# Two-layer attention and gMLP kernel: another order of the start, key features held in SBUF, and small works of a step in another place

## The chip, the cores and the metric

The kernel runs on one core of a Trainium2 chip. The metric is the device time of one execution in microseconds (us); smaller is better. TensorE (PE) multiplies matrices, VectorE (DVE), ScalarE (ACT) and GpSimd (POOL) do elementwise work, SyncE (SP) issues the DMA transfers. PSUM is where TensorE writes.

## What is computed

Two layers, one after the other, each the pair below, with the same weights: a memory-augmented attention and a gMLP mixer, both on a layer-normed input and added to the residual.

```
x = A_x                                     # 1 x 2048 x 640
twice:
    x = x + attention(layernorm(x))
    x = x + gmlp(layernorm(x))

attention: q, k, v = x @ wq, x @ wk, x @ wv      # 32 heads of 20
    M, z = 0, 0
    for s in 4 segments of 512 rows:
        a_dot = softmax(q k^T * 20^-0.5, causal) @ v
        a_mem = (phi(q) @ M) / (phi(q) @ z + 1e-6)    # phi(t) = t + 1 if t > 0 else exp(t)
        o_s = g * a_mem + (1 - g) * a_dot             # g = sigmoid(beta)
        M += phi(k)^T v;  z += sum phi(k)
    return o @ wo

gmlp: z = gelu(x @ w_in)                         # 640 -> 2 x 864
    z1, z2 = halves;  z2 = layernorm(z2)
    g = w_sp @ z2 + b_sp                         # w_sp 2048 x 2048
    return (z1 * g) @ w_out                      # 864 -> 640
```

## The kernel before

**Precision.** A float32 product is done in three fp16 matmuls: each operand is split into a high and a low half (names end in `h` and `l`, or `hl` for both), and high x high, high x low and low x high are added in PSUM. Weights are first scaled by a power of two taken from their largest magnitude: DVE finds the maxima (`wamk`, `wam`), TensorE turns them (`wtp`, L60) and spreads the result over the partitions (`wbc`, L67), and DVE makes the inverse scale `iv` from it (L69 to L74). A split is then an ACT instruction for the high half (L81) and a DVE instruction for the low one (L82), five of each for a weight of 640 rows.

**Stages of the profiled run.** The start, 0 to 60 us (load, scale and split w_v, w_q, w_k; layer norm of the first rows; the first segment's values, L1052; the first unit of queries and keys); attention of layer 0 to about 592; the mixer's first product, L412, and its halves to about 800; the mixer's large product over rows to about 1130; then attention and mixer again to the end.

**Rows.** A tile `t` of 128 rows is prepared by `prep`: load (L1014), statistics (L305 to L308), the subtraction and scaling (L1033), an ACT cast and a low half into `xnhl` (L320, L321), and a DMA that transposes it into `xt` (L322). `value(t)` makes 30 matmuls out of it, in two PSUM tiles `vps`.

**Units.** A unit is six heads (120 columns) of a segment. `unit(s, m)` makes 15 matmuls for its queries (`qps`) and 15 for its keys (`kps`, L1111). `out` then takes the result out of PSUM: the high half (L1125, ACT), the low half (L1129, DVE), both sent to a stack in HBM by DMA (L1226, L1227), from which the scores' operands `qk` are read; and the features phi: `relu` (L1128, ACT), exp written back to the same PSUM bank (L1138, ACT), and the minimum with one plus `relu` (L1143, DVE, for keys; L1141 for queries). Keys' features are split into `phl` (L1152, L1153), transposed by DMA (L1156, `pk`) and go into the memory update `mup` (L1209); DVE masks this into `mst` (L1215). The memory read `num` (L1180) multiplies query features by `mst`. PSUM tiles of values, projections, queries and keys share two banks; the memory's products and the transposed maxima share one more, and the sums `pv` have another.

**Scores.** For a pair of heads TensorE makes scores `mp` for the row maxima (L1246, L1255), DVE reduces them (`mxs`, L1316, L1319), TensorE makes the scores again with the maxima taken off (`es`), ACT takes the exponential into `P` or `Pb` (L1293), ACT casts its high half `PH` (L1328), POOL makes the low half `PL` (L1332), and TensorE multiplies with the values (`pv`, L1366). DVE divides and adds to the memory's part `gm` (L1377 to L1390), and the finished rows go out as `ohl` (L1402).

**Order.** In the attention TensorE's order is written out by steps: `Attention.run` draws matmuls from generators (scores, values `v`, units by their number, projections `p`) in the order of a plan, one list for each segment:

```
plan = ["1v2v3v4v0", "1234vvvv0p", "1p234vvvv0", "1p2p34pppppppp"]
```

`post(k, f)` puts the work of another engine `f` into the list of `k` steps later, in the order of the calls. On the other engines a scheduler sets the order, steered by priorities and by `issue_after`. Each engine runs its own list in order, and SP's transfers share one queue.

Of the kernel before, what the change touches and what calls it, by code (L numbers as in the profile page):

```python
# [19 lines left out]
L = S // NSEG  # L20
# [161 lines left out]
def prologue(g, ctx, wv, wq, wk, wo, w_in, w_out):  # L182
# [7 lines left out]
    with tc.tile_pool(name="wpro", bufs=1, side="right", reuse_waits="tile") as p, \  # L190
# [5 lines left out]
        with tc.high_priority(offset=HP):  # L196
            am = p.tile([128, KD], F32, name="wamk")
            for k in range(KD):
                nc.vector.tensor_reduce(am[:, k:k + 1], st[:, k], AX.X, ALU.max, apply_absolute_value=True)
            nc.vector.tensor_reduce(g.wam[:, 0:1], am, AX.X, ALU.max)  # L200
# [3 lines left out]
        for k in range(KD):  # L204
            e = split_scaled(g, g.w["v"][0][:, k], g.w["v"][1][:, k], st[:, k], 0)
            if k == 2:
                g.third = e
    g.qk_w = wq, wk


def query_key_weights(g, stage, pool, psum, tag):

    nc, tc = g.nc, g.tc
    st = []
    for w, x in zip(g.qk_w, "hl"):
        parts = [g.top[1].tile([128, 2160], F32, tag=f"wi1{x}", name=f"wst{x}1")[:, :3 * D].rearrange("p (k c) -> p k c", c=D),
                 g.top[0].tile([128, 1600], F32, tag=f"wo{x}", name=f"wst{x}2")[:, :2 * D].rearrange("p (k c) -> p k c", c=D)]
        st.append([parts[k // 3][:, k % 3] for k in range(KD)])
        for k in range(KD):
            nc.sync.dma_start(st[-1][k], w[k * 128:(k + 1) * 128, :])  # L220
    for i, nm in ((1, "q"), (2, "k")):
        with tc.issue_after(g.vscale.ins):
            am = pool.tile([128, KD], F32, tag="wamk", name="wamk")
            for k in range(KD):
                nc.vector.tensor_reduce(am[:, k:k + 1], st[i - 1][k], AX.X, ALU.max, apply_absolute_value=True)
# [6 lines left out]
        for k in range(KD):  # L232
            split_scaled(g, h[:, k], l[:, k], st[i - 1][k], i)
        yield

# [102 lines left out]
def phase1b(g, o_d, x, x1_d, z1_d, zh, zl):  # L338

    nc, tc = g.nc, g.tc  # L340
    with ExitStack() as ctx:
# [4 lines left out]
        if not g.wsp_scaled:  # L346
            nc.sync.dma_start(g.bsp, g.b_sp.rearrange("(t p) -> p t", p=128))
        g.wi[0].paired(wp0)
# [68 lines left out]
        g.loaded, g.gelu, g.lo = {}, {}, {}  # L417
# [33 lines left out]
        with tc.high_priority(offset=3 * HP2):  # L451
            a = load(0)
        with tc.high_priority(offset=HP2):
            xn = attn_out(0, *a)
            a = load(ORDER[1])
            th = xn_t(*xn)
        for i, t in enumerate(ORDER):
# [3 lines left out]
            if i + 1 < NT:  # L461
                xn = attn_out(ORDER[i + 1], *a)
# [402 lines left out]
def attn_consts(g, cp, beta):  # L865
# [6 lines left out]
    with tc.tile_pool(name="tmp", bufs=1) as tp, tc.tile_pool(name="acp", bufs=1, space=PSUM) as pp:  # L872
        f = tp.tile([128, 192], F32, name="fmask")
        for t, n, b, sg, op in ((g.eye, 64, 0, 1, ALU.not_equal), (g.step["q"], 192, -64, 1, ALU.is_ge), (g.step["k"], 192, 64, -1, ALU.is_ge)):
            nc.vector.memset(f, 0.0)
            for h in range(2):
                v = f[64 * h:64 * h + 64, :n]
                nc.gpsimd.affine_select(v, v, [[sg, n]], op, BIG if op is ALU.not_equal else -BIG, base=b, channel_multiplier=-sg)
            nc.vector.tensor_copy(t, f[:, :n])
# [7 lines left out]
        nc.vector.tensor_scalar(g.gate, g.gate, 1.0, 0.125, ALU.add, ALU.mult)  # L887

# [29 lines left out]
class Attention:  # L918
# [9 lines left out]
    def __init__(self, g, x, o_d, x1_d):  # L928
# [8 lines left out]
        self.now, self.later, self.half, self.rd = None, {}, {}, set()  # L937
        self.lead = []

    def post(self, k, f, c=None, into=None):  # L940
# [7 lines left out]
        (self.later if into is None else into).setdefault(t, []).append(f)  # L948
# [60 lines left out]
    def prep(self, t):  # L1009
# [4 lines left out]
        nc.sync.dma_start(xt, self.x[t])  # L1014
        ln = []

        def behind():
            ctx = ExitStack()
            for e in (g.hold[:2] or (g.third,)) if t > 1 else ():
# [11 lines left out]
        def last():  # L1031
            mv, rs = ln
            nc.vector.tensor_scalar(xt, xt, mv[:, 0:1], rs, ALU.subtract, ALU.mult)  # L1033
            hl = self.e2.tile([128, 2, D], F16, tag="xh", name="xnhl")
            e = split_t(g, hl, self.xt[s % 2][:, :, :, c], xt, low=nc.vector if g.hold and t in (2, 3) else nc.gpsimd)
            if t == 3:
# [4 lines left out]
    def value(self, t):  # L1041
# [5 lines left out]
        for n in range(2):  # L1047
# [8 lines left out]
            def out(ps=ps.rearrange("p (h d) -> p h d", d=DH), v=self.vs[s % 2][:, t % 4, n * 16:(n + 1) * 16, :]):  # L1056
                nc.scalar.mul(v[:, :, 0:DH], ps, QS)
                nc.vector.scalar_tensor_tensor(v[:, :, DH + 1:], ps, QS, v[:, :, 0:DH], ALU.mult, ALU.subtract)
# [38 lines left out]
    def unit(self, s, m):  # L1097
# [3 lines left out]
        for nm in "qk" if s else "kq":  # L1101
# [12 lines left out]
            self.out(nm, s, m, ps)  # L1114
# [3 lines left out]
    def out(self, nm, s, m, ps):  # L1118
# [18 lines left out]
        def features(r):  # L1137
            nc.scalar.activation(ps, ps, AF.Exp, scale=g.rq if q else g.rk)  # L1138
# [3 lines left out]
            else:  # L1142
                nc.vector.scalar_tensor_tensor(r, ps, 1.0, r, ALU.min, ALU.add)  # L1143
# [54 lines left out]
    def update(self, s, m):  # L1198
# [20 lines left out]
        self.post(1, out)  # L1219

    def stack(self, nm, s, m, hl):
# [6 lines left out]
        if nm == ("k" if s else "q"):  # L1228
# [93 lines left out]
    def cast(self, n, h):  # L1322
# [7 lines left out]
        def low(engine):  # L1330
            for c in (slice(0, 640), slice(640, 1280))[::-1 if n % 2 and h else 1]:
                engine.tensor_tensor(PL[:, c], P[:, h, c], PH[:, c], ALU.subtract)  # L1332

        if h == 0 or n < self.N - self.TAIL:
# [341 lines left out]
```

## Time and profile before

| | |
|---|---|
| runs | 2218.08, 2218.99, 2214.55 us; median 2218.08 |
| profiled execution | 2217.2 us, its span 2215.5 us |
| mean clock granted to TensorE | 0.991 of full speed |
| TensorE busy | 2087.8 us (94%) |
| DVE, ACT, POOL busy | 1625.6, 1250.9, 1402.7 us (73, 56, 63%) |

The span is the time of the profiled execution from the first to the last recorded instruction; some 1.7 us lie around it. A row of the waits gives engine, tile and line that waited, who ended the wait, the total in us, how many times, and the longest. A row of the timeline gives start, duration, engine, line, operation, output and inputs with their shapes, and in brackets the idle time before it and what ended that.

### The profile page before, as it was taken

How to read it: one execution, taken by the hardware profiler on the slowest of the kernel's cores; microseconds unless marked ns; L12 is line 12 of the kernel's file. 1: busy time of each engine (PE TensorE's matmuls, PEld its weight loads, DVE VectorE, ACT ScalarE, POOL GpSimd, SP SyncE). 2: the span in 40 equal slices, each digit the busy share in tenths (PEclk: the TensorE clock that was granted, in tenths of full speed). 3: DMA queues.
4: the chain of work that ended last, by engine and by line, in shares of the span. 5: the costliest groups of instructions: out<-in, count | busy, mean ns of one | idle time of the engine just before them, and what ended most of it. 6: DMA issues, size and time to landing. Idle time of an engine off the chain costs nothing.

```text
span 2215.5 us, 53079 instructions
## 1 busy us (share of the span) xinstructions
PE 2087.8 (94%) x21322; PEld 1265.2 (57%) x21322; DVE 1625.6 (73%) x2889; ACT 1250.9 (56%) x1641; POOL 1402.7 (63%) x1172
## 2 busy tenths in 40 slices
PE   5998888999899999999999989989999999999999
PEld 3555655666545555555555556656665555555555
DVE  7788788788587758888657787787875764675563
ACT  4588788788644433333326987878884433333331
POOL 3387898788645345566414889888894433674660
PEclk9999999999999999999999999999999999999999
DMA  6666557344776686666455456553455335876752
GB/s 177 163 174 184 133 163 197 96 121 126 185 199 182 162 278 171 170 183 178 137 167 131 112 139 153 126 118 90 123 141 145 106 110 185 217 175 171 177 142 82
DMA packets 537703, 342.79 MB, mean 155 GB/s; under 512 B 411600, under 2 KB 463312, under 8 KB 537456
## 3 DMA queue, kind: packets, MB, share of 16 engines
q1 hardware_dynamic: 537456, 339.39, 57.2%
q8 instruction: 167, 2.74, 0.5%
q14 instruction: 80, 0.66, 0.1%
HBM read 159.18 MB, written 92.55 MB: 114 GB/s over the span
## 4 chain that ended last, share of the span: by engine, by line
PE 67%; DVE 14%; ACT 7%; issue 4%; DMA 4%; POOL 3%; SPq 1%; ACTq 0%; DVEq 0%; POOLq 0%
PE ga L670 12%; PE zp L412 11%; PE cyp L706 7%; PE pv L1366 4%; PE qps L1111 4%; PE vps L1052 3%; PE gb L670 3%; PE mp L1255 3%; PE yps L1084 3%; DVE mxs L1319 3%; PE gc L670 3%; PE gd L670 3%; PE kps L1111 2%; PE es L1255 2%; ACT PH L1328 2%
## 5 line engine op out<-in xcount | busy, mean ns | idle before, releaser
L1332 POOL TENSOR_TENSOR PL<-P,PH 128x640 f16<-128x640 f32 x384 | 535.1, 1422 | 86.7 <-PE pv L1366 67.9
L1319 DVE TENSOR_REDUCE mxs<-mp 128x2 f32<-128x1024 f32 (+2 forms) x384 | 320.2, 861 | 123.4 <-PE mp L1246 121.3
L1293 ACT ACTIVATE P<-es,sc 128x1024 f32<-128x1024 f32 (+1 forms) x256 | 271.6, 1061 | 102.0 <-PE es L1246 95.8
L640 POOL TENSOR_TENSOR ts<-ts,wt 128x512 f32<-128x512 f32 x196 | 283.3, 1457 | 11.0
L412 PEld LDWEIGHTS <-th 128*128 128x128 f16 x1920 | 188.0, 98 | 169.6 <-issue 6.9
L1328 ACT CAST PH<-P 128x1280 f16<-128x1280 f32 x192 | 239.7, 1249 | 2.5 <-PE pv L1366 1.0
L670 PEld LDWEIGHTS <-wts 128*128 128x128 f16 x1536 | 150.2, 98 | 134.0 <-issue 5.5
L670 PE MATMUL ga<-zh,wts 128*128 128x432 f16 x768 | 210.8, 346 | 4.5 <-ACT u L737 4.5
L308 POOL TENSOR_TENSOR lnrs<-lnve,mhalf 128x1 f32<-128x1 f32 x96 | 59.8, 631 | 230.2 <-DVE lnve L307 223.1
L1332 POOL TENSOR_TENSOR PL<-Pb,PH 128x640 f16<-128x640 f32 x124 | 175.8, 1447 | 20.3 <-PE pv L1366 19.3
L412 PE MATMUL zp<-wi,th 128*128 128x432 f16 x960 | 181.2, 346 | 3.5 <-ACT z L448 3.5
L640 POOL TENSOR_TENSOR ts<-wt,wt 128x512 f32<-128x512 f16 x28 | 33.9, 1211 | 226.3 <-DMA wt<-wn 226.3
L1052 PE MATMUL vps<-wvh,xt 128*128 128x320 f16 x640 | 154.8, 309 | 23.7 <-DVE relu L1143 13.0
L670 PEld LDWEIGHTS <-wt 128*128 128x128 f16 x1152 | 112.7, 98 | 96.5
L1366 PE MATMUL pv<-vs,PH 128*128 128x41 f16 x2560 | 158.6, 182 | 8.6 <-DVE gm L1387 5.5
L706 PE MATMUL cyp<-wuh,ut 128*128 128x320 f16 (+1 forms) x896 | 163.6, 299 | 2.7 <-DMA ut<-un 1.8
L706 PEld LDWEIGHTS <-ut 128*128 128x128 f16 (+1 forms) x1344 | 131.1, 98 | 57.5 <-DMA ut<-un 4.0
L1255 PEld LDWEIGHTS <-qk 64*128 64x128 f16 (+1 forms) x2048 | 77.9, 94 | 150.1 <-issue 129.3
L1366 PE MATMUL pv<-vs,PL 128*128 128x41 f16 x2560 | 156.3, 181 | 2.6 <-POOL PL L1332 2.6
L412 PE MATMUL zp<-wi1h,th 128*128 128x432 f16 x640 | 149.9, 349 | 2.2 <-DMA th<-xnhl 2.1
L524 DVE SCALAR_TENSOR_TENSOR wn<-wr,wsc,wn 128x512 f16<-128x512 f32 x126 | 92.9, 775 | 76.8 <-ACT wn L523 76.7
L1366 PEld LDWEIGHTS <-PH 128*128 128x128 f16 x2560 | 138.6, 96 | 15.2 <-ACT xnhl L400 2.9
(224 smaller groups left out, 5286.5 us busy)
## 6 DMA issues: line engine op xcount, KB each, us to landing
qk<-st SPq DMA_DIRECT2D x256, 120.0 KB
wr<-in_B_w_sp_dram SPq DMA_DIRECT2D x60, 512.0 KB
z<-z SPq DMA_DIRECT2D x32, 432.0 KB
cz<-z SPq DMA_DIRECT2D x32, 432.0 KB
xt<-in_A_x_dram SPq DMA_DIRECT2D x32, 320.0 KB
st<-khl SPq DMA_DIRECT2D x40, 256.0 KB
st<-qhl SPq DMA_DIRECT2D x40, 256.0 KB
x<-x SPq DMA_DIRECT2D x32, 320.0 KB
```

The source lines that it names most:

```text
L412: nc.tensor.matmul(zp[:, n, :FHH], a[:, k, :], b[:, k, c:c + FHH], start=(k == 0 and j == 0), stop=(k == KD - 1 and j == 2))
L640: nc.gpsimd.tensor_tensor(t, a, t if b == "t" else get(b), ALU.add if op == "+" else ALU.subtract)
L670: nc.tensor.matmul(ps, w[:, a, k % 4, :], z[:, k, j, :], start=start and k == 0 and i == 0, stop=k == NP - 1 and i == 2, skip_group_check= ...
L706: nc.tensor.matmul(yp[:, n, :320], a[:kn[k], k, :], b[:kn[k], k, n * 320:(n + 1) * 320], start=(k == 0 and j == 0), stop=(k == KO - 1 and ...
L1052: nc.tensor.matmul(ps, a[:, k, c], b[:, k, n * 320:(n + 1) * 320], start=(i == 0), stop=(i == 14))
L1111: nc.tensor.matmul(ps, a[:, k, c], b[:, k, :], start=(i == 0), stop=(i == 14))
L1255: nc.tensor.matmul(out[:, h, o:o + w], a[r, ac], b[r, bc], start=o == 0, stop=False, skip_group_check=True)
L1293: g.exp = nc.scalar.activation(P, E, AF.Exp, scale=g.esc)
L1319: e = nc.vector.tensor_reduce(mx[:, :, n, j], mp[:, :, o:o + w], AX.X, ALU.max)
L1328: nc.scalar.copy(PH, P[:, h])
L1332: engine.tensor_tensor(PL[:, c], P[:, h, c], PH[:, c], ALU.subtract)
L1366: nc.tensor.matmul(pv[:, i, h, :41], x[:, c:c + 128], v[:, j, h0 + h, :], start=(j == 0 and x is PH), stop=(j == i and x is PL), skip_grou ...
```

## The change

All parts are in both layers unless it says otherwise.

1. **The start (layer 0 only).** w_q's five row loads go out right behind the second row tile, ahead of the first two transposes, and into the tiles of `P`; w_k's go out behind the fourth row tile. w_v is split by halves of 320 columns. w_q and w_k are split as before in their first 256 columns; the other 384 columns are scaled in place by POOL, cast by ACT and subtracted by POOL. Step mask `k` and the gate's constants are made after w_v's scale. The first unit of a layer makes queries before keys, and the keys' scale is finished inside it.
2. **Key features.** For four units of a layer (those of segments above 0 which the plan lets a `v` or `p` follow), exp goes to an SBUF tile (`exp`, of the three buffers with the tag `hl`), and L1143 reads it there.
3. **Place in the step.** `mst` is put at the head of its step's list; `prep`'s statistics and norm, and the output `ohl`, go to a new list `end`, worked off at the end of a step.
4. **Tail.** The sums `pv` of two of the last three pairs use the memory's bank; the low halves of the last pair are shared by POOL and DVE; the mixer's first two row tiles are loaded ahead of its weights, and their statistics come behind the sums of the fourth and third pair from the end.

The core of the diff:

```diff
@@ prologue
+        for n in range(2):
+            c = slice(n * 320, (n + 1) * 320)
+            for k in range(KD):
+                e = split_scaled(g, g.w["v"][0][:, k, c], g.w["v"][1][:, k, c], st[:, k, c], 0)
...
+def load_rows(g, i):
+    for k in range(KD):
+        g.nc.sync.dma_start(g.qk_raw[i][k], g.qk_w[i][k * 128:(k + 1) * 128, :])
@@ query_key_weights
+    st = g.qk_raw
+    first, rest = slice(0, 256), slice(256, D)
     for i, nm in ((1, "q"), (2, "k")):
-        with tc.issue_after(g.vscale.ins):
+        with tc.issue_after(g.split.ins), tc.issue_after(g.normed[i + 1].ins):
...
-            split_scaled(g, h[:, k], l[:, k], st[i - 1][k], i)
+            split_scaled(g, h[:, k, first], l[:, k, first], st[i - 1][k][:, first], i)
         yield
+    for i, nm in ((1, "q"), (2, "k")):
+        h, l = g.w[nm]
+        for k in range(KD):
+            w = st[i - 1][k][:, rest]
+            nc.gpsimd.tensor_scalar(w, w, g.iv[:, i:i + 1], None, ALU.mult)
+            nc.scalar.copy(h[:, k, rest], w)
+            nc.gpsimd.tensor_tensor(l[:, k, rest], w, h[:, k, rest], ALU.subtract)
@@ phase1b
+        two = [pe2.tile([128, D], F32, tag="x1", name="x1") for _ in range(2)]
+        with tc.high_priority(offset=HP):
+            for t, x1 in zip(ORDER, two):
+                g.loaded[t] = nc.sync.dma_start(x1, x1_d[t])
...
+            with tc.issue_after(g.near[-4].ins):
+                xn = attn_out(0, two[0])
@@ Attention.post
-        (self.later if into is None else into).setdefault(t, []).append(f)
+        todo = (self.later if into is None else into).setdefault(t, [])
+        todo.insert(0 if first else len(todo), f)
@@ Attention.unit
-        for nm in "qk" if s else "kq":
+        for nm in "qk" if s or m == 0 else "kq":
@@ Attention.out
-            nc.scalar.activation(ps, ps, AF.Exp, scale=g.rq if q else g.rk)
+            e = self.u3.tile([128, L], F32, tag="hl", name="exp") if clear else ps
+            nc.scalar.activation(e, ps, AF.Exp, scale=g.rq if q else g.rk)
...
-                nc.vector.scalar_tensor_tensor(r, ps, 1.0, r, ALU.min, ALU.add)
+                nc.vector.scalar_tensor_tensor(r, e, 1.0, r, ALU.min, ALU.add)
@@ the memory update, the low halves, the sums, the output
-        self.post(1, out)
+        self.post(1, out, first=True)
...
+        for i, c in enumerate((slice(0, 640), slice(640, 1280))[::-1 if n % 2 and h else 1]):
+            self.low = (nc.vector if i and n >= self.N - self.TAIL else nc.gpsimd).tensor_tensor(PL[:, c], P[:, h, c], PH[:, c], ALU.subtract)
...
-            pv = self.po.tile([128, 512], F32, tag="pv", name="pv")
+            p, tag = (self.pm, "ms") if n in (self.N - 3, self.N - 1) else (self.po, "pv")
+            pv = p.tile([128, 512], F32, tag=tag, name="pv")
...
-        self.post(2, out)
+        self.post(2, out, into=self.end)
@@ Attention.run
-            for _ in weights:
-                pass
-            yield from self.unit(0, 0)
+            next(weights, None)
+            for i, w in enumerate(self.unit(0, 0)):
+                yield w
+                if i == 6:
+                    next(weights, None)
+                elif i == 20:
+                    for _ in weights:
+                        pass
...
-                        self.post(d, f)
+                        self.post(d, f, into=self.end)
...
+            with self.behind(DVE):
+                for f in self.end.pop(t, ()):
+                    f()
```

What it moves, at three places. Line numbers of the new kernel are other ones.

The start, on SP: `xt` is a row tile or, as DMA_TRANSPOSE, its transpose; `wstv`, `wsth` and `wstl` are w_v, w_q and w_k before the split, in the new kernel `P` and `Pb` hold w_q and w_k; `wst` is a part of wo. Before:

```order
L1014 DMA xt<-in_A_x_dram 128x640
L195 DMA wstv<-in_A_wv_dram 128x640 x5
L1014 DMA xt<-in_A_x_dram 128x640
L883 DMA gate<-in_A_beta_dram 128x32
L277 DMA wst<-in_A_wo_dram 128x640
L347 DMA bsp<-in_B_b_sp_dram 128x16x1
L322 DMA_TRANSPOSE xt_301<-xnhl 128x10x128
L1014 DMA xt<-in_A_x_dram 128x640
L322 DMA_TRANSPOSE xt_301<-xnhl 128x10x128
L1014 DMA xt<-in_A_x_dram 128x640
L220 DMA wsth_452<-in_A_wq_dram 128x640 x3
L220 DMA wsth_453<-in_A_wq_dram 128x640 x2
```

Now:

```order
L1052 DMA xt<-in_A_x_dram 128x640
L195 DMA wstv<-in_A_wv_dram 128x640 x5
L1052 DMA xt<-in_A_x_dram 128x640
L225 DMA P<-in_A_wq_dram 128x640 x5
L905 DMA gate<-in_A_beta_dram 128x32
L298 DMA wst<-in_A_wo_dram 128x640
L368 DMA bsp<-in_B_b_sp_dram 128x16x1
L1052 DMA xt<-in_A_x_dram 128x640
L343 DMA_TRANSPOSE xt_316<-xnhl 128x10x128 x2
L1052 DMA xt<-in_A_x_dram 128x640
L225 DMA P<-in_A_wk_dram 128x640 x3
L225 DMA Pb<-in_A_wk_dram 128x640 x2
```

w_q's loads and the third row tile stand ahead of the first two transposes, and w_k's loads are no longer ahead of the rest of the row tiles but behind the fourth. On TensorE the first unit's 15 key matmuls, which stood ahead of its 15 query matmuls, now follow them, and the small products `wtp` and `wbc` of the keys' and queries' scales stand later among them.

In segment 1 of layer 0, on DVE, at 205 us of the profile (the last of one pair's maxima, then the masked memory). Before:

```order
L1316 TENSOR_REDUCE mxs_304<-mp 128x2x2
L305 BN_STATS lnst<-xt 128x6 x2
L1129 SCALAR_TENSOR_TENSOR khl<-kps,khl 128x512
L1215 TENSOR_TENSOR mst_305<-mup,bmask 128x168
L306 BN_AGGR lnmv<-lnst 128x2
L307 TENSOR_SCALAR lnve<-lnmv 128x1
L1143 SCALAR_TENSOR_TENSOR relu<-kps,relu 128x512
```

Now:

```order
L1357 TENSOR_REDUCE mxs_319<-mp 128x2x2
L1256 TENSOR_TENSOR mst_320<-mup,bmask 128x168
L1169 SCALAR_TENSOR_TENSOR khl<-kps,khl 128x512
L326 BN_STATS lnst<-xt 128x6 x2
L327 BN_AGGR lnmv<-lnst 128x2
L328 TENSOR_SCALAR lnve<-lnmv 128x1
L1184 SCALAR_TENSOR_TENSOR relu<-kps,relu 128x512
```

`mst` has passed the row statistics and the keys' low half.

A little later, on ACT, at 226 to 230 us, where the next unit's keys are followed by a value tile. Before:

```order
L1293 ACTIVATE P<-es,sc 128x2x512
L320 CAST xnhl<-xt 128x640
L1328 CAST PH<-P 128x1280
L1057 ACTIVATE vs_297<-vps 128x16x20
L1402 CAST ohl<-gm 128x640
L1138 ACTIVATE kps<-kps,sc 128x512
L1152 ACTIVATE phl<-relu,sc 128x512
```

Now:

```order
L1334 ACTIVATE P<-es,sc 128x2x512
L1369 CAST PH<-P 128x1280
L1097 ACTIVATE vs_312<-vps 128x16x20
L1179 ACTIVATE exp<-kps,sc 128x512
L341 CAST xnhl<-xt 128x640
L1439 CAST ohl<-gm 128x640
L1193 ACTIVATE phl<-relu,sc 128x512
```

The exp has passed the casts of `xnhl` and `ohl`, and its output is no longer `kps`.

More of the change, by code (lines that the diff above doesn't have):

```diff
@@ L461, in phase1b @@
             if i + 1 < NT:
-                xn = attn_out(ORDER[i + 1], *a)
+                with ExitStack() if i else tc.issue_after(g.near[-3].ins):
+                    xn = attn_out(ORDER[i + 1], *a)
             z2_half(t, w_in_half(1, *th))
@@ L887, in attn_consts @@
         nc.vector.tensor_scalar(g.gate, g.gate, 1.0, 0.125, ALU.add, ALU.mult)
+def attn_consts(g, cp):
+    nc, tc = g.nc, g.tc
+    g.eye = cp.tile([128, 64], F16, name="eye")
+    g.step = {nm: cp.tile([128, 192], F16, name="step" + nm) for nm in "qk"}
+    with tc.tile_pool(name="tmp", bufs=1) as tp, tc.tile_pool(name="acp", bufs=1, space=PSUM) as pp:
+        f = tp.tile([128, 192], F32, name="fmask")
+        for t, n, b, sg, op in ((g.eye, 64, 0, 1, ALU.not_equal), (g.step["q"], 192, -64, 1, ALU.is_ge)):
+            step_mask(g, f, t, n, b, sg, op)
         row = tp.tile([1, 3, 128], F32, name="mrow")
@@ L936, in __init__, with post @@
         self.mem, self.last, self.stacked, self.waiting = False, -1, -1, False
-        self.now, self.later, self.half, self.rd = None, {}, {}, set()
+        self.now, self.later, self.half, self.end, self.rd = None, {}, {}, {}, set()
         self.lead = []
-    def post(self, k, f, c=None, into=None):
+        g.near, g.normed, g.vlow = {}, {}, {}
+    def post(self, k, f, c=None, into=None, first=False):
         if self.now is None:
@@ L1013, in prep @@
         xt = self.e2.tile([128, D], F32, tag="xt", name="xt")
-        nc.sync.dma_start(xt, self.x[t])
+        with self.tc.high_priority(offset=HP) if t in (2, 3) and not g.wo.made else ExitStack(), \
+                self.tc.issue_after(self.second.ins) if t == 3 and not g.wo.made else ExitStack():
+            self.row = nc.sync.dma_start(xt, self.x[t])
         ln = []
@@ L1018, in behind @@
             ctx = ExitStack()
-            for e in (g.hold[:2] or (g.third,)) if t > 1 else ():
+            for e in (g.hold[:2] or (g.kmax if t > 3 else g.third,)) if t > 1 else (g.vmax,) if t and not g.hold else ():
                 ctx.enter_context(self.tc.issue_after(e.ins))
@@ L1422, in early @@
                         a = self.prep(t)
-                    for f in zip(a, self.prep(t + 1)):
+                    b = self.prep(t + 1)
+                    if t and not self.g.wo.made:
+                        with self.tc.high_priority(offset=HP), self.tc.issue_after(self.row.ins):
+                            load_rows(self.g, 1)
+                    for f in zip(a, b):
                         f[0]()
                         f[1]()
+                    if t == 0 and not self.g.wo.made:
+                        query_key_places(self.g, self.Pf, self.Pb)
+                        load_rows(self.g, 0)
             g = self.g
@@ L1466, in run @@
             acc = 0
-            for c in seq:
+            for i, c in enumerate(seq):
                 beg = G * s - LEAD + span * acc / tot
@@ L1484, in run @@
                         continue
-                    it = self.unit(s + (m == 0), m)
+                    it = self.unit(s + (m == 0), m, s > 0 and i + 1 < len(seq) and seq[i + 1] in "vp")
                 acc += w
@@ L1595, in run @@
                 until(t + 1)
+            with self.behind(DVE):
+                for f in self.end.pop(t, ()):
+                    f()
         assert not self.half
-        for t in sorted(self.later):
-            self.now = None
-            for f in self.later[t]:
-                f()
+        self.now = None
+        for left in (self.later, self.end):
+            for t in sorted(left):
+                for f in left[t]:
+                    f()
 def phase1a(g, x, o_d, x1_d, nseg=NSEG):
```

81 lines of the change are left out of this document (36 added, 45 removed).

## The prediction

> **What bounds the kernel now.** I read the page first, then TensorE's waits over the whole run, then busy time by stage, and last the timeline at the places that the diff touches.
>
> ```profile
> span 2215.5 us, 53079 instructions
> PE 2087.8 (94%) x21322; PEld 1265.2 (57%) x21322; DVE 1625.6 (73%) x2889; ACT 1250.9 (56%) x1641; POOL 1402.7 (63%) x1172
> ```
>
> TensorE is busy for 2087.8 of 2215.5 us, and the change takes no matmul of the model away. All it can win lies in the 127.7 us in which TensorE stands still, and in matmuls that run at a lowered clock. The waits of TensorE (total us, times, longest) say who holds it:
>
> ```profile
> PE mp L1255 <- DVE mxs L1319: 14.0, 24, 1.3
> PE vps L1052 <- DVE relu L1143: 13.0, 7, 4.9
> PE es L1255 <- ACT P L1293: 10.3, 17, 1.3
> PE num L1180 <- DVE lnmv L306: 8.3, 4, 2.7
> PE num L1180 <- DVE mst L1215: 5.6, 8, 1.2
> PE pv L1366 <- DVE gm L1387: 5.5, 4, 2.6
> PE es L1255 <- ACT Pb L1293: 3.6, 4, 2.5
> PE yps L1084 <- DVE relu L1143: 2.5, 3, 1.5
> ```
>
> Rows two and eight are a value or projection product that wants the PSUM bank of the key features before it; four and five are the memory read `num` that wants the masked memory `mst`; six and seven are mostly the tails of the attention. The first and third rows, 24.3 us, are the row maxima and the exponentials of the scores, which the change leaves alone. By stage (span, busy us of PE, PEld, DVE, ACT, POOL, then granted clock, DMA share, GB/s):
>
> ```profile
> 0.00:60.00 60.00, 37.02 (x182) 20.35 (x183) 46.03 (x129) 24.08 (x38) 16.89 (x37) 0.91 0.61 174
> 60.00:560.00 500.00, 457.85 (x6971) 294.69 (x6970) 410.86 (x783) 405.33 (x497) 402.69 (x335) 0.98 0.56 151
> 20.00:40.00 20.00, 16.06 (x99) 10.39 (x99) 17.26 (x46) 4.04 (x9) 5.25 (x6) 0.91 0.76 242
> 40.00:60.00 20.00, 15.62 (x66) 6.59 (x65) 13.33 (x36) 12.42 (x19) 1.76 (x2) 0.83 0.35 93
> 220.00:240.00 20.00, 14.94 (x226) 9.92 (x223) 14.15 (x35) 13.13 (x16) 16.00 (x16) 0.83 0.62 150
> 380.00:400.00 20.00, 16.43 (x232) 12.25 (x232) 13.78 (x28) 10.64 (x14) 12.16 (x11) 0.83 0.45 91
> ```
>
> In the attention of layer 0 (60 to 560 us) DVE, ACT and POOL are 82, 81 and 81% busy beside a TensorE of 92%: a wait removed there lets TensorE run into the next one. That row sets how much of a removed wait I count.
>
> **The prologue.** Times in these rows are start and duration; brackets hold the idle time before and what ended it.
>
> ```profile
> 11.61 1.47 SPq L322 DMA_TRANSPOSE xt<-xnhl  x1
> 16.36 0.42 PE L1052 MATMUL vps<-wvh,xt 128*128 128x320 f16 x1 [2.02 <-ACT wvh L81]
> 18.72 3.31 SPq L220 DMA_DIRECT2D wsth<-in_A_wq_dram  x5
> 31.65 0.31 PE L1052 MATMUL vps<-wvh,xt 128*128 128x320 f16 x1 [2.59 <-DMA xt<-xnhl]
> 45.84 1.03 PE L1111 MATMUL kps<-xt,wkh 128*128 128x512 f16 x2 [3.14 <-ACT wkh L81]
> 47.94 0.61 PE L1111 MATMUL kps<-xt,wkl 128*128 128x512 f16 x1 [1.07 <-DVE wkl L82]
> 55.98 0.38 PE L1111 MATMUL qps<-xt,wql 128*128 128x512 f16 x1
> 69.82 1.40 POOL L321 TENSOR_TENSOR xnhl<-xt,xnhl 128x640 f16<-128x640 f32 x1 [27.64 <-ACT xnhl L320]
> L640 POOL TENSOR_TENSOR ts<-ts,wt 128x512 f32<-128x512 f32 x196 | 283.3, 1457 | 11.0
> ```
>
> Now the first unit of queries and keys ends at 56.36 (55.98 + 0.38). The edits there, in order:
> - w_q's five loads move ahead of the first two transposes on SP's queue, and so does the third row load: 6 x 320 KB = 1.97 MB. In 20 to 40 us the queue moved 242 GB/s at a DMA share of 0.76 (third row of the stages), so 6 to 8 us if the transposes had to wait out all of it; but the first was issued at 11.61, when the loads ahead of it were largely through and its product came 4.75 us later. I take +3 us for the first value product, between 0 and +8.
> - Tile 2's transpose no longer queues behind w_k's loads too: the 2.59 goes, -2.6.
> - w_q and w_k are split over their first 256 columns alone on ACT and DVE, and the first unit does queries first, so keys' scale comes later: 3.14 + 1.07 go, -4.2.
> - That stop goes with its slow clock. 40 to 60 us ran at 0.83 of full speed, a loss of 0.17 x 20 = 3.4 us; -3.4, between 0 and that.
> - The scale's second small product (wbc) of the queries' and of the keys' weights now stands between matmuls while DVE still has w_k's maxima and row statistics ahead of it: +1.5, between 0 and 3. The first scores need the keys' stack, now last and behind the second unit's keys on SP: another +1.5, between 0 and 4.
> - The other 384 columns: 20 POOL instructions and 10 ACT casts. No row has this POOL form; by the 1457 ns of 128x512, 384 columns are 1.09 us, 21.9 us in all. POOL stood idle for 27.64 us before 69.82, which is the cover, since columns past 256 are first used by the third unit, behind 60 more matmuls of a unit and a value tile, with scores between. Nothing, then; were POOL later than that unit, each us would be one of TensorE.
> - Step mask, gate constants, halves of w_v: one small load and some short instructions moved off the first 15 us; w_v's twenty ops of 320 instead of ten of 640 split the same elements. About -0.5, inside the rounding.
>
> Sum -4.2; I take -4, between +3 and -8.
>
> **Key features out of PSUM.** Eight units (four a layer) write exp to SBUF, so the bank is free after the exp, not after DVE's `relu`. The worst place:
>
> ```profile
> 226.77 0.68 DVE L1129 SCALAR_TENSOR_TENSOR khl<-kps,khl 128x512 f16<-128x512 f32 x1
> 229.61 0.66 ACT L1138 ACTIVATE kps<-kps,sc 128x512 f32<-128x512 f32 x1
> 230.31 0.69 DVE L1143 SCALAR_TENSOR_TENSOR relu<-kps,relu 128x512 f32<-128x512 f32 x1 [2.62 <-ACT kps L1138]
> 231.05 0.43 PE L1052 MATMUL vps<-wvh,xt 128*128 128x320 f16 x1 [4.90 <-DVE relu L1143]
> ```
>
> TensorE stops at 226.15. In the new ACT order the casts `xnhl` and `ohl` (0.7 us each) come behind the exp, which then ends near 228.4, and the bank is free there: 2.6 of 4.9 us go, 54%. On both relu rows (15.5 us) that is 8.4, between 4 and 13.
>
> `relu` itself now reads two SBUF tiles. The nearest rows are DVE's groups in 60 to 560 us (count | busy us, mean ns):
>
> ```profile
> L1153 DVE SCALAR_TENSOR_TENSOR phl<-relu,sc,phl 128x512 f16<-128x512 f32 x14 | 15.9, 1139 | 0.9 <-ACT phl L1152 0.9
> L1143 DVE SCALAR_TENSOR_TENSOR relu<-kps,relu 128x512 f32<-128x512 f32 x14 | 9.6, 683 | 4.2 <-ACT kps L1138 4.2
> ```
>
> Same shape and operation, both inputs in SBUF: 1139 ns instead of 683. Eight times 0.46 is 3.6 us more of DVE; in a stage where DVE is 82% busy I charge +1 us to TensorE, between 0 and 3.6. [...]
>
> **Memory first, preparation last.**
>
> ```profile
> 204.92 1.23 DVE L1316 TENSOR_REDUCE mxs<-mp 128x4 f32<-128x1024 f32 x1 [1.97 <-PE mp L1246]
> 206.06 0.88 DVE L305 BATCH_NORM_STATS2 lnst<-xt 128x6 f32<-128x320 f32 x2
> 207.44 0.32 DVE L1215 TENSOR_TENSOR mst<-mup,bmask 128x168 f32<-128x168 f32 x1
> 207.91 0.46 PE L1180 MATMUL num<-mst,phq 128*128 128x126 f32 x2 [1.51 <-DVE lnmv L306]
> ```
>
> The wait put down to `lnmv` is one for `mst`, two instructions ahead. In the new order `mst` follows `mxs` at 206.1 and is done at 206.4, when TensorE stops: all of the 1.51 goes. Of 8.3 I count 7.5, and of the 5.6 put down to `mst` a third, 1.8, as there it is mostly behind `mxs` alone. What is late next are the row statistics, `xnhl` and `ohl`; at 231 the tile whose `xnhl` is cast is used a full value tile later, so a few us of delay are covered. Sum -9.3, between -4 and -12.
>
> **Clock.** The stops at 231.05 (4.9) and of `num` (up to 2.7) sit in windows of 0.83, each worth 3.4 us. I count half of the two, -3.4, between 0 and -6.8. [...]
>
> **Tails.**
>
> ```profile
> 579.02 0.89 DVE L305 BATCH_NORM_STATS2 lnst<-x 128x6 f32<-128x320 f32 x2 [4.74 <-DMA x<-x]
> 580.75 0.83 ACT L391 ACTIVATE xn<-x,neg 128x640 f32<-128x640 f32 x1 [3.89 <-DVE neg L390]
> 582.63 0.40 PE L1255 MATMUL es<-qk 64*128 64x384 f16 x4 [2.45 <-ACT Pb L1293]
> 592.24 0.20 PE L1366 MATMUL pv<-vs,PH 128*128 128x41 f16 x1 [2.56 <-DVE gm L1387]
> ```
>
> DVE waited 4.74 us for the mixer's second row tile, ACT stood 3.89 behind it, TensorE 2.45 behind ACT. Loaded ahead of the mixer's weights, the tile is there; and two of the last pairs' sums get a bank of their own, so `pv` need not wait for `gm`. Of 5.5 + 3.6 = 9.1 I count 7, between 3 and 9.
>
> **The sum.** Waits inside the attention are 8.4 + 9.3 + 3.4 = 21.1. Since three engines there are over 80% busy and 24.3 us of other waits stay, I let 60% of it through, 12.7 (between 20%, 4.2, and all). So 4 + 12.7 + 7 - 1 = 22.7 off. The profiled run took 2217.2 us (1.7 more than its span), and the median of the runs, 2218.08, is 0.9 above it: 2217.2 - 22.7 + 0.9 = 2195.4, say 2195. Its own range, by the bounds: all of everything (8 + 21.1 + 9) gives 2180; little (prologue +3, 4.2, tails 3, relu 3.6) gives 2218.
>
> **Rivals.**
> - The waits only move (20%). `mxs` and `P` take back nearly all of the 21.1; prologue and tails stay: 4 + 4.2 + 7 - 3.6 = 11.6 off, 2206. For it: 24 and 17 short waits on `mxs` and `P`, busy shares above 80%. Against: the stops of 4.9 and 2.7 are long beside 1.3.
> - The prologue brings nothing (12%). The transposes wait out w_q's loads (+8), the small products stall by 3 and the first scores by 1.5: -2.6 - 4.2 - 3.4 + 12.5 = +2.3; the rest stands, 2217.2 + 2.3 - 18.7 + 0.9 = 2202. For it: 2.59 us lost to exactly that queueing in the run before.
> - All comes through (8%): 2180.
> - No change (9%): the first two together, 2206 + 6.3 = 2212, or a little worse, to 2220.
> - Slower (11%). The exp tile takes a buffer of the three that rotate under the tag of `khl`, `qhl` and `phl`, so ACT must wait until the DMA that reads the buffer's last content is through, and ACT works in order: `P` of the scores stands behind. The row that decides:
>
> ```profile
> 213.53 1.23 SPq L1156 DMA_TRANSPOSE pk<-phl  x1
> ```
>
>   Three buffers before the exp at 229.61 is the `phl` that this transpose reads, 16 us earlier: against it. Where units stand closer the margin shrinks. Eight stalls of 2.8 us eat the 22.7; at the length of the worst relu wait, 8 x 4.9 = 39, the time is 2195 + 39 x 0.8 = 2226. Below 0.3 us a stall it doesn't show.
>
> **How the numbers follow.** The forecast has 40%. A change under 0.2% (4.4 us) can't be told from none in this kernel, so faster means below 2213.6: forecast, the first three rivals, 40 + 20 + 12 + 8 = 80%, of which I leave 2 points to no change for the forecast's weak end: 78, 11, 11. The range leaves out the slow rival and half of no change above, and the last of "all comes through" below: 2178 to 2216.
>
> **What would show it.** Prologue: first value product at 19 to 20, no stop near 32 or 46, first unit done at 50 to 53. Features: no wait of `vps` on `relu`, the stop at the place of 231.05 near 2.3, `relu` at 0.7 to 1.9 us. Memory: no `num` behind `lnmv`. Tail: ACT's `xn` without 3.89 before it. Rows of `mp` behind `mxs` and `es` behind `P` grow from 24.3 to about 33. I am wrong if ACT shows idle time before exp that a DMA ends, if the first value product comes after 24, or if those two rows grow by 20.

## The result, and the profile after

The changed kernel takes 2189.45 us (median of 4 runs, 2187.46 to 2192.22), the kernel before on the same chip 2218.53: a ratio of 0.9871, with a 95% interval of 0.9857 to 0.9886, or 29 us less. The forecast was 2195, with 2178 to 2216 as its range. The profiled execution took 2187.46 us. The page of the changed kernel, the two rows that answer to those of before:

```profile
span 2185.7 us, 53146 instructions
PE 2073.5 (95%) x21322; PEld 1258.9 (58%) x21322; DVE 1632.4 (75%) x2894; ACT 1251.7 (57%) x1656; POOL 1426.6 (65%) x1192
```

With the same 21322 matmuls TensorE is busy 14.3 us less and stands still 15.5 us less (127.7 to 112.2). The busy time fell because less of it ran at a lowered clock: the profiled execution of the kernel before had nine stretches at half speed (granted clock 0.50), 41.0 us together, that of the changed kernel has one of 6.8 us. So about half of the gain came through the clock. The four runs of the changed kernel were granted 0.995 to 0.998 of full speed, and the profiled one is at the upper end. Its waits in the changed kernel (not shown are 7.0 for the scale of w_v at the very start and 4.4 of the mixer's large product, 8.4 and 4.5 before, and smaller ones):

```profile
PE mp L1296 <- DVE mxs L1360: 17.2, 26, 1.4
PE es L1296 <- ACT P L1334: 9.4, 16, 1.1
PE zp L438 <- DMA th<-xnhl: 8.6, 9, 1.8
PE vps L1092 <- DMA xt<-xnhl: 7.4, 1, 7.4
PE pv L1402 <- POOL PL L1372: 7.3, 9, 1.6
PE vps L1092 <- ACT exp L1179: 5.9, 4, 2.2
PE num L1221 <- DVE mst L1256: 5.5, 8, 0.8
PE vps L1092 <- DVE relu L1184: 3.3, 4, 1.3
PE wbc L67 <- DVE wdg L64: 3.0, 2, 2.3
```

`num` behind `lnmv` (8.3) and `pv` behind `gm` (5.5) are gone. Of 15.5 us behind `relu`, 9.2 are left, now mostly put down to `exp`. The wait for the first transpose, 7.4, is new. Three others grew: for `PL` from 2.6 to 7.3, for the small product of a scale from 0.6 to 3.0, and that of the mixer's first product `zp` for its transposed rows `th` from 2.1 to 8.6. The mixer's other wait of before, behind `z`, is gone:

```profile
PE zp L412 <- ACT z L448: 3.5, 2, 2.4
PE zp L412 <- DMA th<-xnhl: 2.1, 3, 1.3
```

The waits on `mxs` and `P`, 24.3 before, are 26.6: they grew by 2.3, not by the 9 that the prediction expected. Stages of the changed kernel:

```profile
0.00:60.00 60.00, 35.97 (x196) 20.46 (x197) 47.61 (x136) 27.29 (x55) 36.14 (x55) 1.00 0.63 182
60.00:560.00 500.00, 464.96 (x7196) 301.22 (x7196) 421.20 (x800) 414.60 (x508) 418.94 (x349) 0.99 0.59 155
220.00:240.00 20.00, 17.05 (x237) 11.43 (x236) 16.70 (x36) 15.63 (x22) 17.91 (x16) 0.83 0.57 144
380.00:400.00 20.00, 18.69 (x285) 13.27 (x282) 15.30 (x34) 14.75 (x19) 16.01 (x13) 1.00 0.50 117
```

DVE, ACT and POOL are now 84, 83 and 84% busy in the attention, with room still for 225 matmuls more in the same 500 us. Near 220 the clock is still lowered once; near 40 and 380 it no longer is.

From the 161st value matmul to the end of layer 0's attention, and in layer 1's behind its first unit, TensorE's order is the same in both kernels, so the start of the n-th matmul of a tile in one trace can be held against the same one in the other. The lead so worked out, in us:

| at | before | after | lead | gained here | forecast |
|---|---|---|---|---|---|
| 161st value matmul, start over | 82.50 | 79.49 | 3.0 | 3.0 | 4 |
| 301st projection matmul, layer 0 nearly over | 572.59 | 557.47 | 15.1 | 12.1 | |
| first `zp`, tail over | 593.63 | 576.20 | 17.4 | 2.3 | |
| 481st value matmul, second layer begins | 1133.87 | 1115.43 | 18.4 | 1.0 | |
| 661st projection matmul, layer 1 nearly over | 1659.08 | 1629.53 | 29.6 | 11.1 | both attentions 11.7, here 23.2 |
| 961st `zp`, its tail over | 1676.56 | 1647.39 | 29.2 | -0.4 | |
| last `cyp` | 2210.99 | 2181.23 | 29.8 | 0.6 | tails 7, here with the mixers 3.5 |

So the two attentions brought twice what was forecast for them, and the tails with the mixers behind them half.

### The profile page after: what moved, and what is told of

Read it like the earlier page. It is cut to its first block, busy times and chain, and to the rows that moved or that the text cites. A ratio compares the mean times of both kernels' runs of the same rounds, so it can differ in the third digit from the quotient of the medians.

```text
span 2185.7 us, 53146 instructions
## 1 busy us (share of the span) xinstructions
PE 2073.5 (95%) x21322; PEld 1258.9 (58%) x21322; DVE 1632.4 (75%) x2894; ACT 1251.7 (57%) x1656; POOL 1426.6 (65%) x1192
## 4 chain that ended last, share of the span: by engine, by line
PE 68%; DVE 13%; ACT 6%; DMA 5%; POOL 3%; issue 3%; SPq 1%; ACTq 0%; DVEq 0%; POOLq 0%
PE zp L438 13%; PE ga L695 12%; PE cyp L731 7%; PE qps L1151 4%; PE pv L1402 4%; PE gb L695 3%; PE yps L1124 3%; PE mp L1296 3%; PE vps L1092 3%; DVE mxs L1360 3%; PE gc L695 3%; PE gd L695 3%; POOL PL L1372 2%; PE kps L1151 2%; PE es L1296 2%
## 5 line engine op out<-in xcount | busy, mean ns | idle before, releaser
L1372 POOL TENSOR_TENSOR PL<-P,PH 128x640 f16<-128x640 f32 x384 | 537.2, 1428 | 81.2 <-PE pv L1402 62.6
L438 PEld LDWEIGHTS <-th 128*128 128x128 f16 x1920 | 187.0, 98 | 171.6 <-DMA th<-xnhl 11.9
L1092 PE MATMUL vps<-wvh,xt 128*128 128x320 f16 x640 | 150.4, 304 | 18.3 <-DMA xt<-xnhl 7.4
L1296 PE MATMUL mp<-qk 60*128 60x512 f16 (+3 forms) x1024 | 126.0, 303 | 23.6 <-DVE mxs L1360 17.2
```

Of the source, the lines that this page charges most:

```text
L438: nc.tensor.matmul(zp[:, n, :FHH], a[:, k, :], b[:, k, c:c + FHH], start=(k == 0 and j == 0), stop=(k == KD - 1 and j == 2))
L1092: nc.tensor.matmul(ps, a[:, k, c], b[:, k, n * 320:(n + 1) * 320], start=(i == 0), stop=(i == 14))
L1296: nc.tensor.matmul(out[:, h, o:o + w], a[r, ac], b[r, bc], start=o == 0, stop=False, skip_group_check=True)
L1372: self.low = (nc.vector if i and n >= self.N - self.TAIL else nc.gpsimd).tensor_tensor(PL[:, c], P[:, h, c], PH[:, c], ALU.subtract)
```

## Experiments

Differences below are from the ratios to the kernel before, times 2218. Each ratio has an interval of some 3 to 5 us either way, so a difference below that is none that can be measured.

**Taking one part out of the changed kernel.** Key features back into PSUM:

```diff
-            self.out(nm, s, m, ps, clear and nm == "k")
+            self.out(nm, s, m, ps, False)
```

> The changed kernel, but exp of the key features goes back into the PSUM bank for all units. Theory 1 (each removed wait brings its whole length, and the clock window behind it as well): TensorE's waits on relu grow again by about 7 us, half-speed windows come back for some 3 to 5 us of lost work, so about 2201 us (2197 to 2205). Theory 2 (the prediction's: only 60% passes, and the clock is a small term): 8.4 x 0.6 = 5 us, about 2194.5.

2193.33 us, ratio 0.989 (0.9866 to 0.9913): 4 us slower than the changed kernel, at the edge of what can be measured. At the units that the part frees, the waits of value and projection products grew from 5.9 to 11.1 us, not to the 14.1 of before: exp stays ahead of the casts here, so the longest stop is 2.86 us and not 4.90. The loss fits theory 2. The middle of theory 1, 2201, lies outside the interval, though its lower end, 2197, doesn't.

`mst`, preparation and `ohl` back to their old places:

```diff
-        self.post(1, out, first=True)
+        self.post(1, out)
...
-        self.post(2, out, into=self.end)
+        self.post(2, out)
...
-                        self.post(d, f, into=self.end)
+                        self.post(d, f)
```

> The changed kernel, but mst, the preparation and the output ohl stand where they stood before. Theory 1: the 8.3 us of num behind lnmv come back in full and the half-speed window at about 380 us too (3.4 us), about 2201 us (2197 to 2205). Theory 2: 9.3 x 0.6 = 5.6 us, about 2195.

2206.47 us, ratio 0.9947 (0.993 to 0.9965): 17 us slower, three times the prediction's term and more than either theory gave. In its trace `num` waits as before, exp stands behind both casts again at the place of the longest stop (4.24 us), and 37.5 us run at half speed:

```profile
PE num L1221 <- DVE lnmv L327: 8.5, 4, 2.7
PE num L1221 <- DVE mst L1256: 5.7, 8, 1.2
```

The attention's tail as it was (`pv` in one bank, the last low halves and the mixer's row loads as before; the diff is the reverse of part 4):

> The changed kernel, but the attention's tail as before (pv in one bank, old shares of the last low halves, the mixer's row tiles loaded behind its weights). Theory 1 (from the lead of the changed kernel along TensorE's order: 2.3 us gained in the tail of layer 0, 1.0 in layer 1, 1 more in the mixer): about 2194 us (2191 to 2196). Theory 2 (the prediction's 7 us): 2196.5.

2194.24 us, ratio 0.9897 (0.9875 to 0.9918): 5 to 6 us slower. The two theories are 2.5 us apart and the interval is 9.5 us wide, so the time doesn't tell them apart. The trace has `pv` behind `gm` back with 5.4 us and `zp` behind `z` with 3.6, but only 2.6 for `PL` and 2.1 for `th`. On balance TensorE stands still just 1.3 us longer in it than in the changed kernel; it is busy 4.9 us longer, with 17.1 us at half speed instead of 6.8. So in these two executions the part worked mostly through the clock, not through the waits that it removes.

**Which half of that part.** Only the head of the list taken back, and only the end list taken back:

```diff
# a_nofirst
-        self.post(1, out, first=True)
+        self.post(1, out)
# a_noend
-        self.post(2, out, into=self.end)
+        self.post(2, out)
...
-                        self.post(d, f, into=self.end)
+                        self.post(d, f)
```

> The changed kernel, but mst keeps its old place in its step's list; preparation and ohl stay at the step's end. Theory 1 (the end list is what frees num, since the row statistics no longer stand ahead of mst): only the key's low half, 0.6 us, stands ahead of mst at some of the twelve waits of num, 2 to 4 us with no new half-speed window, about 2192.5. Theory 2 (the head of the list is what counts): most of the 17 us lost without both come back, 2200 or more.

2199.29 us, ratio 0.9913 (0.9894 to 0.9931): 9 us slower.

> The changed kernel, but preparation and ohl stay in the lists where they were; mst stays at the head of its list. Theory 1: num waits no longer, but exp of the key features stands again behind the casts of xnhl and ohl (1.4 us at two or three places a layer), with a half-speed window or two: 4 to 8 us, about 2195. Theory 2 (the head of the list does it alone): within 2 us of 2189.5.

2189.71 us, ratio 0.9873 (0.9852 to 0.9893): no change. The end list brings nothing that can be measured once `mst` is first; it makes up for some of the loss where `mst` isn't, and there too exp is ahead of the casts. The reason that theory 1 gave for a loss didn't occur: without the end list exp still stays ahead of the casts at the place of the longest stop. Waits of `num` in `a_nofirst`, where the key's low half stands ahead of `mst`:

```profile
PE num L1221 <- DVE mst L1256: 11.9, 12, 2.9
377.06 0.46 PE L1221 MATMUL num<-mst,phq 128*128 128x126 f32 x2 [2.88 <-DVE mst L1256]
```

**The part alone on the kernel before**, first both halves, then the one line:

```diff
# b_first: the kernel before with
-        self.post(1, out)
+        self.post(1, out, first=True)
...
-        (self.later if into is None else into).setdefault(t, []).append(f)
+        todo = (self.later if into is None else into).setdefault(t, [])
+        todo.insert(0 if first else len(todo), f)
# b_place: this and the end list
```

> The kernel before with this part alone: mst at the head of its list, preparation and ohl in the end list. Theory 1 (the parts add up: 17 us were lost when this part was taken out of the changed kernel): 12 to 17 us off, about 2203. Theory 2 (the part's value rests on the key features being out of PSUM): 6 us off or less, 2212 or more.

2202.05 us, ratio 0.9925 (0.9908 to 0.9941): 17 us off.

> The kernel before with one line of the change: mst goes to the head of its step's list; preparation and ohl stay where they were. Theory 1 (this line is the larger part of the whole change, as its removal from the changed kernel cost 10 us and the end list's nothing): 12 to 17 us off, 2201 to 2206, num no longer behind lnmv, and no half-speed window near 209 and 383 us. Theory 2 (it needs the end list to be worth that much): 10 us off or less, 2208 or more.

2201.59 us, ratio 0.9921 (0.9907 to 0.9935): 17.5 us off with the one line, some 60% of the whole change. How a wait of 2.65 us turns into more is seen at one place: the same `num` in the kernel before (first row; the stage of 380 to 400 us had 16.43 busy at a clock of 0.83) and here, the matmul and the stage:

```profile
384.01 0.77 PE L1180 MATMUL num<-mst,phq 128*128 128x126 f32 x2 [2.65 <-DVE lnmv L306]
381.32 0.46 PE L1181 MATMUL num<-mst,phq 128*128 128x126 f32 x2 [0.80 <-DVE mst L1216]
380.00:400.00 20.00, 18.28 (x273) 13.79 (x272) 16.31 (x34) 15.00 (x18) 17.48 (x15) 1.00 0.68 124
```

By the starts of the same matmuls, this kernel's lead is 0.8 us at 367, 2.7 at this `num` and 5.5 six microseconds later, as the kernel before runs its next 6.8 us at half speed. At 425 us the lead is still 5.6: nothing took it back.

The line does more than end the wait of `num`. Without the end list and without exp in SBUF, ACT's order at the longest stop has changed as well: exp (here the row that writes `kps`) is ahead of the cast of `xnhl`, and of `ohl` too, and the stop of 4.90 us is 2.87.

```profile
226.51 0.65 ACT L1139 ACTIVATE kps<-kps,sc 128x512 f32<-128x512 f32 x1
227.07 0.72 ACT L320 CAST xnhl<-xt 128x640 f16<-128x640 f32 x1
227.93 0.30 PE L1053 MATMUL vps<-wvh,xt 128*128 128x320 f16 x1 [2.87 <-DVE relu L1144]
```

ACT's order is the scheduler's; why it follows from this line was not traced. In the profiled executions TensorE stands still 11.9 us less than before, of which the four waits behind `lnmv` are 8.3, and is busy 3.2 us less.

**Key features alone on the kernel before:**

> The kernel before with this part alone: exp of the key features of four units a layer in SBUF. Theory 1 (the part is worth what its removal cost, 3.9 us): about 2214.5. Theory 2 (without the end list the exp keeps its place behind the casts of xnhl and ohl, so at the stop of 4.9 us only the relu's 0.7 us goes): 0 to 2.5 us off, 2216 to 2218.

2213.24 us, ratio 0.9979 (0.9967 to 0.999): 4.7 us off (2.2 to 7.3), near theory 1; the upper end of theory 2, 2.5, is not excluded. At the place of the longest stop almost nothing goes, as theory 2 said,

```profile
228.18 0.72 ACT L320 CAST xnhl<-xt 128x640 f16<-128x640 f32 x1 [0.94 <-DVE xt L1033]
230.31 0.71 ACT L1403 CAST ohl<-gm 128x640 f16<-128x640 f32 x1
230.92 0.69 ACT L1139 ACTIVATE exp<-kps,sc 128x512 f32<-128x512 f32 x1
231.66 0.42 PE L1052 MATMUL vps<-wvh,xt 128*128 128x320 f16 x1 [4.25 <-ACT exp L1139]
```

since both casts still stand ahead of exp: 4.25 for 4.90. What theory 2 left out are the other freed units: together their waits fall from 14.1 to 8.3 us, as the projection products (2.5) wait no longer and two stops of 2.0 are halved. The parts add up nearly: 17 + 4 to 5 + 5 to 6 (tail, by removal) leave 1 to 3 us for the start, whose lead is 3.0.

**Does the clock's part of it cost time everywhere?** Seven extra matmuls, whose result isn't used, fill the one stop of the changed kernel that still lowers its clock:

```diff
+            if t == 8 and n == 1:
+                spare = self.pm.tile([128, 512], F32, tag="ms", name="spare")
+                for r in range(7):
+                    nc.tensor.matmul(spare, wh[:, 0, 0:128], wh[:, 1, 0:512], start=True, stop=True)
             ps = self.pd.tile([128, L], F32, tag="dn", name="vps")[:, :320]
```

> The changed kernel, with seven extra matmuls of 512 columns (0.22 us each, result not used) on TensorE ahead of the second half of the ninth value tile in each layer, where it stands still for 2.1 us behind exp. They lie inside the stop and lengthen nothing. Theory 1 (the clock is halved by idle time inside a fixed window of 3.4 us, so filling the stop keeps it): no half-speed window near 222 or 1302 us, 2 to 5 us less than the changed kernel, about 2186. Theory 2 (the clock follows something else, as the stop's length to its end, or the fill only delays): 2189.5 to 2193.

2191.73 us, ratio 0.9876 (0.9856 to 0.9897): no gain. The clock did what theory 1 said, the time didn't. From its trace, the fill, the wait after it, and the stage:

```profile
220.04 1.68 PE L1091 MATMUL spare<-wvh 128*128 128x512 f16 x7
222.31 0.30 PE L1096 MATMUL vps<-wvh,xt 128*128 128x320 f16 x1 [0.58 <-ACT exp L1183]
233.80 0.40 PE L1300 MATMUL mp<-qk 60*128 60x384 f16 x4 [2.67 <-DVE mxs L1364]
220.00:240.00 20.00, 15.99 (x246) 10.79 (x244) 18.79 (x35) 15.78 (x21) 18.25 (x15) 1.00 0.66 144
```

The clock is 1.00 instead of 0.83 and TensorE is 1.9 us ahead at 228; at 233.80 it waits 2.67 us for `mxs`, where the changed kernel waits 0.54, and the lead is gone. DVE is busy for 18.79 of these 20 us. Not all of DVE's lateness was there before, though: four tiny instructions ahead of this `mxs` (L70, L71, L74, L314) took 3.96 us together, and 2.41 in the changed kernel. So DVE took the lead back in this run; that it would have done so whatever the fill does to these instructions isn't shown.

**The start.** w_q's loads behind the first two transposes:

```diff
-                        load_rows(self.g, 0)
+                        with self.tc.issue_after(self.second.ins):
+                            self.wq = load_rows(self.g, 0)
...
-                        with self.tc.high_priority(offset=HP), self.tc.issue_after(self.row.ins):
+                        with self.tc.high_priority(offset=HP), self.tc.issue_after(self.row.ins), self.tc.issue_after(self.wq.ins):
```

> The changed kernel, but w_q's five loads leave SP behind the first two transposes instead of ahead of them, w_k's behind those. Theory 1 (the 7.39 us that TensorE waits for the first transpose are a loss of the change and reach the end): first value product near 16 us instead of 19.9, and 2 to 3 us off, about 2187. Rival (the scales of w_q on DVE set the end of the start): the wait of the small product wbc grows from 2.3 to 5 us or more, and the time stays at 2189.5.

2191.18 us, ratio 0.9883 (0.9858 to 0.9909): no gain. The first value product came at 16.00, but TensorE then stood 3.99 us at 31.39 for the third transpose: the wait moved, not to the small product that the rival named, but along the same queue. So w_k's loads went behind the third transpose too, and its statistics were freed:

```diff
+            if t == 2:
+                self.thirdt = e
...
+                    if t and not self.g.wo.made:
+                        with self.tc.high_priority(offset=HP), self.tc.issue_after(self.thirdt.ins):
+                            load_rows(self.g, 1)
...
-            for e in (g.hold[:2] or (g.kmax if t > 3 else g.third,)) if t > 1 else (g.vmax,) if t and not g.hold else ():
+            for e in (g.hold[:2] or (g.kmax if t > 3 else g.third if t > 2 else g.vscale,)) if t > 1 else (g.vmax,) if t and not g.hold else ():
```

> The changed kernel, with w_q's loads behind the first two transposes, w_k's behind the third, and the third row tile's statistics free to run as soon as w_v's scale is made. Theory 1 (what TensorE waits for in the start is only the order on the queue of transfers): first value product at 16, the wait at the third tile below 3 us, the first unit done near 49 instead of 52.6, about 2186. Rival (the sum of bytes and DVE's scales set the end, the wait moves on to the small product or to the split of w_q): first unit done at 52 to 53, 2189.5.

2192.36 us, ratio 0.9883 (0.9865 to 0.99): no gain either. Its trace:

```profile
15.15 0.45 PE L1094 MATMUL vps<-wvh,xt 128*128 128x320 f16 x1 [3.18 <-DMA xt<-xnhl]
25.99 0.31 PE L1094 MATMUL vps<-wvh,xt 128*128 128x320 f16 x1 [0.40 <-DMA xt<-xnhl]
40.29 0.59 PE L1153 MATMUL qps<-xt,wqh 128*128 128x512 f16 x2 [2.06 <-DVE vs L1100]
46.45 0.39 PE L1153 MATMUL kps<-xt,wkl 128*128 128x512 f16 x1 [1.59 <-DVE wkl L82]
48.37 0.50 PE L1153 MATMUL kps<-xt,wkl 128*128 128x512 f16 x1 [1.10 <-DVE wkl L82]
```

The third tile is no longer waited for, and a lead of 4 us shrinks to 2.0 at the first query product, to 0.1 at the first value product after the unit: the rows show DVE's `vs` and its splits of w_k taking it, and the clock is at half speed for 3.4 us from 48.5. Both together, extra matmuls and this start:

> The extra matmuls and the reordered start together, on the changed kernel. Theory 1 (the start's gain at the third tile was lost again to a half-speed window at 48 us, by chance of where it fell): 2184 to 2187. Theory 2 (the start is held by the scales on DVE, whatever the transfers): as with the extra matmuls alone.

2192.36 us, ratio 0.9878 (0.986 to 0.9896), again with 3.4 us at half speed from 50.5. Theory 1 falls as far as its number goes; what holds the start is only partly shown, as DVE's work of the two scales was not changed by itself. No version beats the changed kernel.

## Why the prediction was right, and where it was off

- **Direction, size and range held.** 29 us came for a forecast of 23, by the parts that were named, but in other shares, and the misses partly cancel: the memory brought far more than its term, the start and the tails less. That the total lies so near is in part luck. The slow rival (exp waits for a buffer) didn't appear: ACT never stood idle before one of the eight exps. `mxs` and `P` took back 2.3 us, neither the 9 expected nor the 20 that would have meant a wrong account.
- **Start: 4 forecast, 3.0 measured, by other terms.** The first value product came at 19.91, 3.6 us later than before for the 3 taken:

```profile
11.28 3.64 SPq L1052 DMA_DIRECT2D xt<-in_A_x_dram  x1
14.96 3.20 SPq L343 DMA_TRANSPOSE xt<-xnhl  x2
19.91 0.45 PE L1092 MATMUL vps<-wvh,xt 128*128 128x320 f16 x1 [7.39 <-DMA xt<-xnhl]
```

  The third row tile's load, ahead of the transposes, sat in SP for 3.64 us, and they followed at 14.96 instead of 11.61. The stop near 32 and the slow clock went, and the small product stalled 2.28 us, within its bounds; the split of w_k still stopped TensorE for 2.6 us, of the 4.2 that I had struck out. POOL's rest columns took 23 us for the 21.9 taken, from 38.4 to 64.5, and TensorE never waited for them.
- **Features: 8.4 before the discount, 4 to 5 measured.** At the units that are freed the waits fell from 14.1 to 5.9 us, by 58% for the 54% taken from the worst place, where the stop was forecast at 2.3 and is 2.16. The rest of the 9.2 us left, 3.3, stands behind units that the change doesn't free; they had 1.3 before. What the prediction had wrong is whose gain this is: with exp in PSUM the freed units' waits are 11.1 in the changed kernel and 11.3 with `mst` moved alone, so 3 of the 8.2 us come from exp passing the casts, which the line for `mst` brings by itself (and the end list, where `mst` isn't first), and 5 from SBUF. `relu` on two SBUF tiles is dearer than the 1139 ns taken: the eight take 10.5 us, 5 more than from PSUM, for the 3.6 expected. DVE's groups in 60 to 560 us:

```profile
L1184 DVE SCALAR_TENSOR_TENSOR relu<-kps,relu 128x512 f32<-128x512 f32 x9 | 6.1, 682 | 0.1
L1184 DVE SCALAR_TENSOR_TENSOR relu<-exp,relu 128x512 f32<-128x512 f32 x4 | 5.5, 1371 | 1.8 <-ACT exp L1179 1.8
```

  The means are 682 ns from PSUM and 1371 with both inputs in SBUF, in one run; the eight of the whole run took 0.84 to 1.96 us, and what makes them longer isn't shown. `PL` on POOL took 1428 ns on average, for 1422 before.
- **Memory first: the step that was mis-sized.** I put 9.3 on it and let 60% through. It brought 17. (`mst` stands one instruction ahead of `lnmv`, not two; of the two `num` rows all 8.3 behind `lnmv` went, and nothing of the 5.6 put down to `mst`.) Three things were wrong. The discount, taken from busy shares of a whole stage, does not hold for the wait of 2.65 us near 384: the 1.85 us of it that went passed whole. Its clock stood as a term of its own, -3.4, cut in half and then discounted again; behind 384 us the clock alone brought 2.8 us in one layer, and over the whole kernel TensorE's busy time fell by 14.3, where the prologue's and this term were 3.4 each. And exp's place ahead of the casts, which I had counted with the features, comes with this line. The busy share was right at the other place, near 222, where the fill's gain was taken back within 6 us, in part by DVE instructions that took longer there. One share for all waits was the mistake: at these two places it was decided by what the next engine was doing then.
- **Tails: 7 forecast, 3.5 by the lead with the mixers (5 to 6 by removal).** The wait behind `gm` went, and that of `es` behind `Pb` fell from 2.45 to 0.69, as ACT stood 2.14 us instead of 3.89 before `xn`. POOL became the next:

```profile
562.80 0.20 PE L1402 MATMUL pv<-vs,PL 128*128 128x41 f16 x1 [1.07 <-POOL PL L1372]
565.78 0.39 PE L1296 MATMUL es<-qk 64*128 64x384 f16 x4 [0.69 <-ACT Pb L1334]
570.69 0.19 PE L1402 MATMUL pv<-vs,PL 128*128 128x41 f16 x1 [1.57 <-POOL PL L1372]
```

  `PL` was in the list of before with 2.6 us and I did not ask what would be late next there. Nor did I ask it of the mixer, whose product `zp` now waits 8.6 us for `th`, where it waited 2.1 for it and 3.5 for `z`. So the waits that went were replaced almost in full, and what the part brought came mostly through the clock (as the run without it shows above).

## What to carry to other kernels

Look for the shortest instruction that a busy engine runs too late: 0.3 us of `mst`, moved ahead of its neighbours in DVE's list, was worth 17 of 29 us, more than the new start, the freed bank and the tail together. Part of that came from another engine's order, which the scheduler changed with it, so measure a line alone before crediting its neighbours. Price each wait by the engine that would be late next at that very place, not by a stage's busy share. Ask of a lowered clock, too, whether another engine would stop TensorE right behind it. Moving one transfer forward in a shared queue moved the wait here (7.39 us at the first transpose in one order, 3.99 at the third in the other), so it must be followed until the end of the stage.

## What the runs showed of the hardware

- **Half speed followed idle time within fixed windows of 3.413 us.** In all fourteen traces every half-speed stretch inside the run begins a whole multiple of 3.413 us from the others of its trace and lasts 3.41 or 6.83 us. I divided the traces into these windows, from where the record of the clock begins, and took those that ran at full speed. With less than 1.25 us of idle time of TensorE in them, 1 of 8547 was followed by half speed, with 1.25 to 2 us 17 of 201, and with 2 us or more 54 of 55; in the traces of the kernel before and the changed one alone it is 0 of 1221, 2 of 30 and 8 of 8. Of two stops in the changed kernel, the one of 2.16 us that ends at 221.74 lies inside one window, and half speed followed; the one of 2.14 that ends at 1301.82 is split between two, 1.06 and 1.08 us, and it didn't. With the extra matmuls in the first of them, the clock from 220 to 240 us was 1.00 instead of 0.83.
- **Some tiny DVE instructions took seven to nine times what they took in another trace.** Three on 128 x 4 or fewer numbers, in the trace with the extra matmuls:

```profile
228.06 1.38 DVE L70 TENSOR_SCALAR pw<-pw 128x4 int32<-128x4 int32 x1
229.48 1.30 DVE L71 TENSOR_TENSOR pw<-pw,floor 128x4 f32<-128x4 f32 x1
231.01 1.13 DVE L314 TENSOR_SCALAR sc<-pw 128x2 f32<-128x2 f32 x1
```

  In the changed kernel the first two took 0.16 and 0.15 us, the third 1.06; there another one (L74, 128 x 4), 0.15 here, took 1.04. They are part of why DVE was late there; what makes them longer isn't shown.
